# Gated linear attention with a squared-ReLU mixer on one core: the same operations in another order, from two new tables of plan positions

## The chip, the cores and the metric

The kernel runs on one core of one Trainium2 chip. The metric is the device time of one execution in microseconds (us). Before the change three executions took 425.59, 427.54 and 427.96 us, a median of 427.54. One more execution was taken with the hardware profiler; it took 424.87 us, and its trace has a span of 423.0 us.

## The reference

Two layers follow each other. The first is a linear attention whose state decays with a complex gate, for 4 batches, 8 heads, 768 positions and a head size of 48:

```python
mag = np.sqrt(a_re * a_re + a_im * a_im)
scale = np.minimum(mag, 0.999) / (mag + 1e-06)
for t in range(S):
    S_re, S_im = ar * S_re - ai * S_im + k[t] v[t]^T, ar * S_im + ai * S_re
    y[:, :, t] = q[t] @ S_re
```

The second takes the attention's output `x` (768 positions of 384 features for each batch):

```python
x_prev = x shifted by one position
xk, xr = mu_k * x + (1 - mu_k) * x_prev, mu_r * x + (1 - mu_r) * x_prev
k = np.maximum(xk @ w_k, 0.0)            # 384 -> 1024
v = k * k @ w_v                          # 1024 -> 384
out = v / (1.0 + np.exp(-(xr @ w_r)))    # 384 -> 384
```

All is float32.

## The kernel before

**Units.** A batch is cut into two halves of 384 positions, which gives eight units u = 0 to 7. A unit goes through three groups of steps.

- *gate(u)* loads the gate, k and q in three pieces of 128 features (`g`, line 673) and v (`v`, line 682). ScalarE (ACT) and VectorE (DVE) turn the gate into a log magnitude and a phase, sum both along the positions and multiply k and q by the results. ACT needs two of its function tables for it (exponential and logarithm, then arctangent and sine) and a third for the sigmoid later on; each change is an ACT_TABLE_LOAD (line 304). The last products of a gate are `g<-g,r` on DVE (line 808).
- *attend(u)* does the attention in chunks of 128 positions. SyncE (SP) copies k and q of each head from `g` into a head's own tile (`kq`, line 845; unit 0 also uses `x`). TensorE (PE) turns k round (`tr`, line 876), ACT copies that out (`kt`, line 882), PE makes the state's increments (`up`, line 896), DVE adds them up (lines 901 and 903). PE makes the scores (`sc`, line 925), DVE masks them (`pt`, line 934), and PE makes the output of a pair of heads (`y`, lines 960 and 966), which ACT copies out (`ys`, line 975) and SP moves into the mixer's input (`xt`, line 981).
- *mix(u)* takes differences of neighbours (`dx`, line 417) and mixes them (`xm`, line 435; for unit 0 straight into `x`, line 425). A float32 operand goes through PE as a high and a low part, three products in the place of one: ACT makes the high part (`x`, line 443), DVE the low (line 446). `z` (line 464) is the product with w_k or w_r; ACT takes ReLU (`r`, line 500) and the square (`h`, line 504), ACT or DVE the square's high part (`hhi`, line 326), DVE its low (`hlo`, line 512); `o` (line 531) is the product with w_v, added up over eight steps j. DVE multiplies by the gate (line 553) and SP stores. Unit 0 uses undivided float32 weights and operands in the place of the parts: `z` on line 459 and `o` on line 528.

**Weights** come in ten pieces in a packed form (`raw`, line 384), ACT or DVE takes the exponent out (line 600), DVE shifts and joins (lines 606 and 610), and after unit 0's use they are split into high and low parts (`w`, lines 633 and 636). All ten loads are needed for unit 0, the later steps j last.

**Looks.** Each of the 19 weight blocks is loaded once more (`again`, line 649) into a single buffer, DVE masks it (line 653), and ACT measures it (lines 655 and 656); the sums decide at the end whether a slow path has to run. As there is one buffer, the load of a look cannot begin before ACT has ended the look before it.

**Fillers.** While PE has nothing ready early in the program, the order holds small products of the identity (`warm`, line 1019). Their number is fixed when the program is built.

**What sets the order.** All operations are first recorded, with an estimated cost, in a `Plan`. `AT` holds for each unit's attend and mix a stretch on a line of plan time, over which its PE operations are spread evenly (`steps`); `SHIFTS` moves the due times of everything that is not on PE, one number for each call of `run`. `due` works back from PE's places to a due time for each operation; `Plan.run` then plays the plan through, and at each moment each engine takes, of the operations that could start, the one that is due first:

```python
i = min((i for i in queue if can(i)), default=None,
        key=lambda i: (due[i] + self.STAY * (e == "PE" and ops[i]["kind"] != kind), i))
```

The instructions are written out in the order in which the plan took them. On the chip each engine's queue, SP's too, runs strictly in that order: an instruction that waits holds up all behind it on its engine. In the same way all transfers are issued from SP, one after another. Which of ACT and DVE makes a `hhi`, or takes out an exponent, is also decided in the play.

Of the kernel before, what the change touches and what calls it, by code (L numbers as in the profile page):

```python
# [41 lines left out]
CAP = 0.999  # L42


AT = ((0.0, 16.0), (6.28, 13.76), (7.74, 9.08), (13.58, 23.34), (8.72, 9.63), (16.36, 26.91), (19.37, 20.41), (27.64, 32.72),
      (27.54, 33.34), (28.23, 33.79), (27.95, 29.17), (65.85, 145.98), (25.53, 63.88), (108.62, 138.07), (34.95, 105.45), (30.5, 41.58))
SHIFTS = (9.3, 16.4, 21.7, 11.3, 10.8, -22.0, 2.7, 0.8, 22.0, -13.5, 2.3, 36.2, 2.3, -15.3,
          12.9, 19.7, -32.6, 0.0, 0.5, 0.5, 1.2, -6.4, 0.0, 0.2, -54.6, 2.7, 50.3, 46.6)
PAIRS = 0, 3, 1, 2
PIECE = 2  # L50
GP = 2
# [234 lines left out]
def tile_kernel(ctx, tc, gat, vt, w_all, mu, slow_g, slow_v, out):  # L286
# [275 lines left out]
    with ExitStack() as fast:  # L562
# [460 lines left out]
        n = range(len(pieces))  # L1023
        shifts = iter(SHIFTS)
        run(gate(0), 0, 0, next(shifts))
# [3 lines left out]
        for u in range(NU):  # L1029
            run(attend(u), *AT[2 * u], next(shifts))  # L1030
            run(mix(u, (x0, x0_slot) if u == 0 else None), *AT[2 * u + 1], next(shifts))
            if u == 0:
# [151 lines left out]
```

## Time and profile before

| | |
|---|---|
| three executions, us | 425.59, 427.54, 427.96 (median 427.54) |
| profiled execution, us | 424.87 |
| its span, us | 423.0 |
| busy in the span, us | PE 379.8, weight loads 346.9, ACT 350.0, DVE 329.0 |
| moved by DMA | 69.92 MB, 16 engines busy 55% of the span on the kernel's queue |
| table loads on ACT | 22 |

The profile's page has the busy share of each engine in 40 slices, the chain of waits that ended last, and the costliest groups. The view of waits names for each engine the operation that waited, the one it waited for, the total, the number of times and the longest. The view of stretches gives busy time of each engine between two moments. PE's records of a plain float32 product are two for one matmul, so 82 records of `warm` are 41 fillers.

### The profile page before, as it was taken

What the parts mean: (1) busy time and instruction counts of PE and PEld (TensorE: products, weight loads), DVE (VectorE), ACT (ScalarE), POOL (GpSimd) and SP (SyncE); (2) the same over time, 40 slices, a digit from 0 to 9 for tenths busy, and PEclk for the clock granted to TensorE, in tenths of its full rate; (3) what the DMA queues carried; (4) which work ended last, traced back from release to release, by engine and by line L of the source; (5) the groups of instructions that cost most, each with busy time, mean ns of one, the idle gap of its engine ahead of it and who ended that gap; (6) DMA issues with size and microseconds to landing.
All of it is one profiled execution on the core that took longest, in us unless ns stands there. A gap on an engine that the chain in (4) does not pass through costs nothing.

```text
span 423.0 us, 9454 instructions
## 1 busy us (share of the span) xinstructions
PE 379.8 (90%) x3655; PEld 346.9 (82%) x3655; DVE 329.0 (78%) x522; ACT 350.0 (83%) x635; POOL 6.3 (1%) x40
## 2 busy tenths in 40 slices
PE   1007999999999999999999999999999999999993
PEld 1007985676779998999999998998899999999992
DVE  6799889988699989699979787959978865356421
ACT  5899979686999899899998999889999954675431
POOL 3000000000000000000000000000001000000000
PEclk9999999999999999999999999999999999999998
DMA  7958899249727555594659363846442635314101
GB/s 277 416 209 186 277 313 288 59 125 297 169 59 245 174 134 143 150 325 123 112 153 332 92 166 100 278 174 146 129 113 84 142 94 150 102 40 130 39 2 64
DMA packets 28661, 69.92 MB, mean 165 GB/s; under 512 B 5696, under 2 KB 11840, under 8 KB 28608
## 3 DMA queue, kind: packets, MB, share of 16 engines
q1 hardware_dynamic: 28608, 69.23, 55.3%
q8 instruction: 31, 0.51, 0.5%
q14 instruction: 22, 0.18, 0.2%
HBM read 40.90 MB, written 4.72 MB: 108 GB/s over the span
## 4 chain that ended last, share of the span: by engine, by line
PE 67%; ACT 13%; DMA 10%; DVE 6%; SPq 2%; issue 1%; DVEq 0%; ACTq 0%
PE z L464 26%; PE o L531 16%; PE sc L925 6%; PE y L960 5%; PE up L896 4%; PE y L966 4%; DMA g<-in_gat 3%; PE tr L876 3%; DMA raw<-in_w_all 2%; PE z L459 2%; PE o L528 2%; DMA again<-in_w_all 2%; ACT r L310 2%; DVE g L808 2%; ACT L304 2%; DMA xt<-ys 1%
## 5 line engine op out<-in xcount | busy, mean ns | idle before, releaser
L464 PE MATMUL z<-x,w 128*128 128x384 f32 x693 | 133.3, 340 | 0.0
L464 PEld LDWEIGHTS z<-x,w 128*128 128x128 f32 x693 | 120.3, 188 | 1.8 <-issue 1.2
L531 PE MATMUL o<-hhi,w 128*128 128x384 f32 x336 | 87.4, 341 | 0.0
L531 PEld LDWEIGHTS o<-hhi,w 128*128 128x128 f32 x336 | 60.0, 188 | 0.8 <-issue 0.5
L531 PE MATMUL o<-hlo,w 128*128 128x384 f32 x168 | 56.8, 338 | 0.9 <-DVE hlo L512 0.9
L876 PE MATMUL tr<-ident,g 128*128 128x128 f32 x120 | 19.4, 287 | 30.6 <-DVE g L808 30.6
L808 DVE TENSOR_TENSOR g<-g,r 128x768 f32<-128x768 f32 x48 | 42.8, 953 | 5.1 <-ACT r L310 4.8
L500 ACT ACTIVATE r<-z 128x384 f32<-128x384 f32 x64 | 30.8, 484 | 19.0 <-PE z L464 17.4
L876 PEld LDWEIGHTS tr<-ident,g 128*128 128x128 f32 x120 | 14.0, 144 | 33.3 <-DVE g L808 31.6
L925 PEld LDWEIGHTS sc<-kq 112*64 112x64 f32 x744 | 33.4, 137 | 3.6 <-issue 3.2
L925 PE MATMUL sc<-kq 112*64 112x64 f32 (+1 forms) x744 | 36.0, 249 | 0.0
L504 ACT ACTIVATE h<-r 128x384 f32<-128x384 f32 x64 | 33.1, 523 | 0.8
L934 DVE TENSOR_TENSOR pt<-sc,masks 128x512 int32<-128x512 int32 x48 | 31.3, 684 | 2.2 <-PE sc L925 2.2
L531 PEld LDWEIGHTS o<-hlo,w 128*128 128x128 f32 x168 | 31.5, 188 | 1.5 <-DVE hlo L512 1.5
L310 ACT ACTIVATE sq<-m 128x1152 f32<-128x1152 f32 (+2 forms) x30 | 27.9, 967 | 5.6 <-DVE m L756 5.6
L512 DVE TENSOR_TENSOR hlo<-h,hhi 128x384 fp32r<-128x384 f32 x56 | 30.4, 553 | 2.0 <-ACT hhi L326 0.5
L304 ACT ACT_TABLE_LOAD x22 | 28.2, 1283 | 1.1 <-PEq L1173 0.8
L446 DVE TENSOR_TENSOR x<-xm,x 128x384 fp32r<-128x384 f32 x42 | 23.2, 552 | 5.9 <-ACT x L443 5.9
L960 PE MATMUL y<-pt,v 128*64 128x128 f32 (+1 forms) x384 | 27.3, 276 | 0.0
L435 DVE SCALAR_TENSOR_TENSOR xm<-dx,mu_sb,xt 128x384 f32<-128x384 f32 x42 | 25.5, 615 | 0.9
L653 DVE TENSOR_SCALAR again<-again 128x384 uint8<-128x384 uint8 x19 | 11.5, 608 | 18.9 <-DMA again<-in_w_all 15.9
L443 ACT CAST x<-xm 128x384 fp32r<-128x384 f32 x42 | 21.0, 513 | 6.3 <-PE z L464 3.2
(85 smaller groups left out, 644.2 us busy)
## 6 DMA issues: line engine op xcount, KB each, us to landing
g<-in_gat SPq DMA_DIRECT2D x18, 768.0 KB, 6.2
kq<-g SPq DMA_DIRECT2D x94, 144.0 KB, 3.4
again<-in_w_all SPq DMA_DIRECT2D x19, 384.0 KB, 3.3
raw<-in_w_all SPq DMA_DIRECT2D x9, 768.0 KB, 8.7
v<-in_vt SPq DMA_DIRECT2D x24, 288.0 KB, 4.7
g<-in_gat SPq DMA_DIRECT2D x12, 384.0 KB, 6.7
out_t<-zr SPq DMA_DIRECT2D x24, 192.0 KB, 2.1
xt<-ys SPq DMA_DIRECT2D x48, 72.0 KB, 3.1
```

Source lines behind the costliest of these rows:

```text
L304: nc.scalar.add_instruction(mybir.InstLoadActFuncSet(name=nc.get_next_instruction_name(), act_func_set_id=loaded[0], engine=mybir.EngineTy ...
L310: nc.scalar.activation(out=out, in_=in_, func=func, **kw)
L464: nc.tensor.matmul(z, lhsT=wt[s[0]][:, part, s[1]], rhs=r[which][:, ct], start=n == 0, stop=n == 3 * NT - 1)
L500: nc.scalar.activation(out=t["r", j], in_=t["f", j], func=AF.Relu)
L504: nc.scalar.activation(out=t["h", j], in_=t["r", j], func=AF.Square)
L512: nc.vector.tensor_tensor(out=t["lo", j], in0=t["h", j], in1=t["hi", j].bitcast(F32), op=ALU.subtract)
L531: nc.tensor.matmul(tiles["o", mt], lhsT=wt[W_V + 2 * j][:, part, ts(mt, P)], rhs=r, start=j == 0 and n == 0, stop=j == NJ - 1 and n == 2)
L808: nc.vector.tensor_tensor(out=g[:, ct, 2 * i:2 * i + 2], in0=g[:, ct, 2:4], in1=t["r"][:, ct, 1 - i:2 - i].to_broadcast([P, 2, U]), op=ALU ...
L876: nc.tensor.transpose(out=t["tr", c, part][:, ct * P:(ct + 1) * P], in_=G[u][:, ct, 2 * part, c * P:(c + 1) * P], identity=ident)
L925: nc.tensor.matmul(sc[rows, i, cols], lhsT=kq[2 * p + j][:, 0, c * P + late * Q:][:, :Q], rhs=q if j else q[:, ::-1], start=True, stop=True)
L934: nc.vector.tensor_tensor(out=pts[k, c].bitcast(I32), in0=both, in1=masks.unsqueeze(1).to_broadcast([P, 2, 2, P]), op=ALU.bitwise_and)
L960: nc.tensor.matmul(t["y", p][rows, ts(c, P)], lhsT=V[u][c][:, cols], rhs=w, start=c == 0, stop=False)
```

## The change

Only the two tables of numbers are replaced. All operations, sizes, buffers and estimated costs stay as they are. The numbers were found by a search that took as its measure the mean over replays in which transfers land late by random amounts; those before went by the plan's length.

```diff
-AT = ((0.0, 16.0), (6.28, 13.76), (7.74, 9.08), (13.58, 23.34), (8.72, 9.63), (16.36, 26.91), (19.37, 20.41), (27.64, 32.72),
-      (27.54, 33.34), (28.23, 33.79), (27.95, 29.17), (65.85, 145.98), (25.53, 63.88), (108.62, 138.07), (34.95, 105.45), (30.5, 41.58))
-SHIFTS = (9.3, 16.4, 21.7, 11.3, 10.8, -22.0, 2.7, 0.8, 22.0, -13.5, 2.3, 36.2, 2.3, -15.3,
-          12.9, 19.7, -32.6, 0.0, 0.5, 0.5, 1.2, -6.4, 0.0, 0.2, -54.6, 2.7, 50.3, 46.6)
+AT = ((3.46, 6.82), (0.08, 10.89), (1.48, 1.99), (12.28, 20.43), (8.51, 12.78), (15.29, 21.97), (16.79, 17.69), (18.73, 25.2),
+      (21.73, 28.63), (22.46, 28.96), (20.36, 23.11), (71.92, 148.9), (21.27, 76.59), (101.4, 131.96), (58.71, 126.27), (37.6, 56.94))
+SHIFTS = (15.7, 108.1, 129.2, 35.2, 23.3, 17.2, -12.5, 37.4, 6.1, 0.4, -29.4, -0.4, 4.5, 0.0,
+          4.8, -5.6, -5.6, 1.2, -6.5, -1.4, 3.9, 6.0, -62.0, -11.1, -30.6, -1.6, 76.5, 5.6)
```

What it moves is seen in the engines' orders. The fillers go from 55 to 52; 41 of them stood in one row ahead of unit 0's first `z`, and 33 stand there now. Of the `hhi`, 22 were on DVE and 24 are now. The number of table loads is the same. Three places follow.

**SP, from the last moves of unit 0's k and q to the loads ahead of unit 1's.** `raw` are weight pieces, `g` the gate pieces of unit 2, `xt` the parts of unit 0's attention output, `v` values, `kq` unit 1's k and q. Before:

```order
L384 DMA raw<-in_w_all 128x6144 x2
L981 DMA xt<-ys 48x384 x2
L981 DMA xt<-ys 32x384
L981 DMA xt<-ys 16x384
L673 DMA g<-in_gat 128x1536
L981 DMA xt<-ys 16x384
L981 DMA xt<-ys 32x384
L673 DMA g<-in_gat 128x1536 x2
L981 DMA xt<-ys 48x384 x4
L682 DMA v<-in_vt 128x576 x3
L384 DMA raw<-in_w_all 128x6144 x3
```

Now:

```order
L384 DMA raw<-in_w_all 128x6144 x2
L673 DMA g<-in_gat 128x1536
L981 DMA xt<-ys 48x384 x2
L981 DMA xt<-ys 32x384
L981 DMA xt<-ys 16x384 x2
L981 DMA xt<-ys 32x384
L673 DMA g<-in_gat 128x1536
L981 DMA xt<-ys 48x384 x4
L673 DMA g<-in_gat 128x1536
L682 DMA v<-in_vt 128x576 x3
L384 DMA raw<-in_w_all 128x6144
```

The last four moves of `xt` have two pieces of `g` ahead of them in the place of three. The last two weight pieces are issued after the 14 moves of unit 1's first heads (`kq`), no longer ahead of them.

**ACT, between the sigmoid of unit 0 and unit 3's gate.** The table load is the one back to the exponential's table, after the last sigmoid (`zr<-zr`) of unit 0; `kt` are the copies for unit 2's state, two for each chunk. Before:

```order
L882 COPY kt<-tr 128x8x48 x2
L443 CAST x<-xm 128x384 x2
L482 COPY zr<-z 128x384
L633 CAST w<-raw 128x2x384
L310 ACTIVATE zr<-zr 128x384
L304 ACT_TABLE_LOAD
L310 ACTIVATE m<-m,consts 128x1152
L633 CAST w<-raw 128x2x384
L310 ACTIVATE ph,stat<-m 128x1152
L443 CAST x<-xm 128x384
L882 COPY kt<-tr 128x8x48
L633 CAST w<-raw 128x2x384
```

Now:

```order
L882 COPY kt<-tr 128x8x48 x2
L443 CAST x<-xm 128x384 x2
L633 CAST w<-raw 128x2x384
L482 COPY zr<-z 128x384
L882 COPY kt<-tr 128x8x48 x2
L443 CAST x<-xm 128x384
L633 CAST w<-raw 128x2x384
L310 ACTIVATE zr<-zr 128x384
L304 ACT_TABLE_LOAD
L310 ACTIVATE m<-m,consts 128x1152
```

The second chunk's two copies stand ahead of the table load and of the gate's two long functions.

**DVE, at the end of unit 6.** `again` are the looks, `hhi` and `hlo` the parts of the squares that unit 6's `o` reads, `x`, `xm` and `dx` the making of unit 7's operands. Before, from one look to the next but one:

```order
L653 TENSOR_SCALAR again<-again 128x384
L446 TENSOR_TENSOR x<-xm,x 128x384
L435 SCALAR_TENSOR_TENSOR xm<-dx,mu_sb,xt 128x384
L326 CAST hhi<-h 128x384
L512 TENSOR_TENSOR hlo<-h,hhi 128x384
L653 TENSOR_SCALAR again<-again 128x384
L446 TENSOR_TENSOR x<-xm,x 128x384
L435 SCALAR_TENSOR_TENSOR xm<-dx,mu_sb,xt 128x384
L417 TENSOR_TENSOR dx<-xt 128x384
L446 TENSOR_TENSOR x<-xm,x 128x384
L512 TENSOR_TENSOR hlo<-h,hhi 128x384
```

Now, from the look at the same place:

```order
L653 TENSOR_SCALAR again<-again 128x384
L446 TENSOR_TENSOR x<-xm,x 128x384
L435 SCALAR_TENSOR_TENSOR xm<-dx,mu_sb,xt 128x384
L446 TENSOR_TENSOR x<-xm,x 128x384
L435 SCALAR_TENSOR_TENSOR xm<-dx,mu_sb,xt 128x384
L326 CAST hhi<-h 128x384
L417 TENSOR_TENSOR dx<-xt 128x384
L512 TENSOR_TENSOR hlo<-h,hhi 128x384
L446 TENSOR_TENSOR x<-xm,x 128x384
L435 SCALAR_TENSOR_TENSOR xm<-dx,mu_sb,xt 128x384
L512 TENSOR_TENSOR hlo<-h,hhi 128x384
```

Four instructions stood between that look and the next; now twelve do (the last two are not shown), and the parts for two steps of `o` (`hlo`) are among them.

## The prediction

> **What bounds the kernel now.** I read the page first, then the stretches, then the waits of TensorE (PE), and last the timelines at the places where PE waits.
>
> ```profile
> span 423.0 us, 9454 instructions
> PE 379.8 (90%) x3655; PEld 346.9 (82%) x3655; DVE 329.0 (78%) x522; ACT 350.0 (83%) x635; POOL 6.3 (1%) x40
> ...
> PE tr L876 <- DVE g L808: 30.6, 3, 26.8
> PE up L896 <- ACT kt L882: 1.9, 3, 0.9
> PE o L531 <- DVE hlo L512: 0.9, 2, 0.4
> PE o L528 <- ACT h L504: 0.5, 1, 0.5
> PE z L459 <- DVE x L425: 0.4, 1, 0.4
> ...
> PE tr L876 <- DVE g L808: 0.3, 1, 0.3
> ```
>
> PE is the fullest engine, and three quarters of its idle time is one wait: the first `tr` waits until ACT and DVE have made unit 0's gate. The other waits come to 0.3 + 1.9 + 0.9 + 0.5 + 0.4 = 4.0 us (0.3 is the last row, the same wait asked for after 60 us alone; the rest of its 30.6 lies at the start). By stretches (columns: from:to, length, busy PE, weight loads, DVE, ACT, POOL, granted clock, DMA share, GB/s):
>
> ```profile
> 34.00:61.50 27.50, 27.40 (x393) 26.54 (x394) 24.71 (x37) 24.71 (x52) 0.00 (x0) 1.00 0.86 256
> 61.50:119.00 57.50, 56.51 (x476) 37.60 (x474) 50.70 (x73) 48.69 (x78) 0.24 (x1) 1.00 0.67 185
> 119.00:280.00 161.00, 159.80 (x1629) 152.49 (x1630) 139.11 (x221) 150.45 (x267) 0.73 (x2) 1.00 0.61 179
> 280.00:303.00 23.00, 21.94 (x217) 20.62 (x216) 20.17 (x34) 22.33 (x41) 0.00 (x0) 1.00 0.45 106
> 303.00:374.00 71.00, 71.00 (x708) 68.07 (x707) 47.82 (x82) 54.06 (x109) 1.96 (x13) 1.00 0.43 115
> 374.00:386.00 12.00, 11.15 (x62) 10.51 (x61) 7.60 (x16) 7.58 (x18) 0.00 (x0) 1.00 0.22 66
> 416.00:423.00 7.00, 0.00 (x0) 0.00 (x0) 0.45 (x2) 0.00 (x0) 0.00 (x0) 0.75 0.29 97
> ```
>
> From 34 us on PE is busy nearly without a break, until 416; then 7 us of end follow. So the time is 34 us of start, the work of PE, what PE loses inside, and 7 us. An order changes neither the work nor the end. The new order does not change the start either: ACT's order is the same up to the Exp of unit 1's gate, and DVE's up to the second of the six `g<-g,r` of unit 0, after which one join (`raw`, line 610) stands in the place of two shifts. What can be won lies inside: the 4.0 us of waits, and the fillers, which count as busy:
>
> ```profile
> 34.58 1.49 PE L1019 MATMUL warm<-ident 128*128 128x128 f32 x6
> ...
> 52.25 9.42 PE L1019 MATMUL warm<-ident 128*128 128x128 f32 x82
> ```
>
> 82 records in 9.42 us are 0.115 us each, or 0.23 us a filler.
>
> **Term A: from the first attention output to unit 0's first products.** The 41 fillers from 52.25 stand for a wait: unit 0's first `z` (line 459) needs `x` on DVE (line 425), that needs `dx` (line 417), and that the last moves of `xt`.
>
> ```profile
> 45.98 2.45 SPq L981 DMA_DIRECT2D xt<-ys  x4
> ...
> 50.48 2.00 SPq L673 DMA_DIRECT2D g<-in_gat  x2
> 53.83 3.15 SPq L981 DMA_DIRECT2D xt<-ys  x4
> ...
> DMA to landing us min/median/max: 4.9/5.5/6.9
> ...
> 52.15 8.28 DMA g<-in_gat
> ...
> 61.14 1.03 DVE L417 TENSOR_TENSOR dx<-xt 128x384 f32<-128x384 f32 x2 [1.08 <-DMA v<-in_vt]
> ...
> xt<-ys SPq DMA_DIRECT2D x48, 72.0 KB, 3.1
> ```
>
> These ten moves of 24 to 72 KB took 4.9 to 6.9 us to land; the median of the whole run is 3.1 for the 72 KB ones. The last two `dx` began at 61.14, 0.7 us after the third piece of `g` (768 KB, 52.15 + 8.28 = 60.43) had landed. The name beside the wait is v's; I take it to be the last `xt`, which DVE needs, and v it does not. The change puts that piece of `g` behind the four moves. Of 5.5 us of landing I take 2 off, towards the 3.1 (5.5 - 3.1 = 2.4 at most): `dx` then begins near 59. The order agrees: it has eight fillers fewer in that row and five more ahead of it, three fewer in all, 0.7 us.
>
> The Trainium skill has the rule for it (DMA: Bandwidth & Descriptors, Queues, rings and completion order): on each DMA engine the descriptors of a ring are consumed in the order of the ring. By that rule a piece of `g` issued later could not delay these moves at all, and they would gain the piece's whole time. The landings of 4.9 to 6.9, against 3.1 elsewhere, fit it.
>
> With `x` earlier, the two waits behind it go: `z` L459 (0.4) because `dx` comes 2 us earlier against 0.7 fewer fillers, and `o` L528 (0.5) because the order now puts unit 1's first two `tr` between unit 0's third `z` and its first `o`. That is 0.7 + 0.4 + 0.5 = 1.6. The weight loads ahead of the same two products waited longer:
>
> ```profile
> PEld z L459 <- DVE x L425: 1.3, 2, 1.0
> PEld o L528 <- ACT h L504: 1.1, 1, 1.1
> PEld o L531 <- DVE hlo L512: 1.5, 2, 0.8
> ```
>
> With 1.3 and 1.1 it is 3.1. I take 1.9, near the lower, as a wait of a weight load is partly under the matmul before it. Bounds: 0 (if `x` comes no earlier, fewer fillers only make a longer wait) to 3.1.
>
> **Term B: the copies for unit 2's state.**
>
> ```profile
> 113.44 1.28 ACT L304 ACT_TABLE_LOAD   x1
> 114.74 1.26 ACT L310 ACTIVATE m<-m,consts 128x1152 f32<-128x1152 f32 x1
> 116.62 1.16 ACT L310 ACTIVATE ph<-m 128x1152 f32<-128x1152 f32 x1
> 119.28 0.47 ACT L882 COPY kt<-tr 128x384 f32<-128x384 f32 x1
> ...
> 119.81 1.13 PE L896 MATMUL up<-v,kt 128*64 128x48 f32 x32 [0.86 <-ACT kt L882]
> ```
>
> The copies now stand ahead of 1.28 + 1.26 + 1.16 us of table load and gate. PE in turn asks for `up` earlier: unit 0's last four operations `o`, some 4 us of PE's work, now stand behind it. ACT's copies come by the three long ones and one split (0.8) earlier, 4.5 us, so the wait of 0.86 goes. Bounds: 0, and 0.86; I take 0.9. The other two of the three waits for `kt` I leave.
>
> **Term C: the looks.**
>
> ```profile
> DVE again L653 <- DMA again<-in_w_all: 15.9, 9, 3.6
> ...
> 377.29 0.61 DVE L653 TENSOR_SCALAR again<-again 128x384 uint8<-128x384 uint8 x1 [2.97 <-ACT x L443]
> ...
> 380.50 0.44 PE L531 MATMUL o<-hlo,w 128*128 128x384 f32 x1 [0.43 <-DVE hlo L512]
> 382.77 0.44 PE L531 MATMUL o<-hlo,w 128*128 128x384 f32 x1 [0.42 <-DVE hlo L512]
> ```
>
> DVE waited 15.9 us in nine looks whose load was not there. Mostly that costs nothing. At 374.3 it did: DVE stood 2.97 us at a look, the `hlo` behind it came late, and PE lost 0.43 + 0.42 there (1.5 by the weight loads). In the new order both `hlo` stand ahead of the next look. I take 1.2, between 0.9 and 1.5; bounds 0 and 1.5.
>
> At 280 to 303 PE lost 23.00 - 21.94 = 1.06, behind two more waits of DVE for looks. One of the two looks stands where it stood; the other's load is now issued ahead of three loads of v. I take 0.3, bounds 0 and 1.06.
>
> **Term D: new waits.** Elsewhere PE asks earlier than before: for unit 1's outputs `y` (6.8 us of PE's work earlier), for unit 2's (8.1), unit 3's first `tr` (2.3), while DVE's producers come 4.6, 5.0 and 0 us earlier in DVE's own order (both counted by the operations that changed sides, at their mean times). From 119 to 280 ACT has 150.45 busy of 161 and DVE 139.11, so neither has much to catch up with. Nothing in the trace prices this; bounds are 0 and once more all small waits of today, 4.0. I take 1.0: DVE's 22 free us there are near enough.
>
> **Sum.** -1.9 - 0.9 - 1.2 - 0.3 + 1.0 = -3.3 us. On the profiled execution: 424.87 - 3.3 = 421.6 (span 419.7, with the same 1.9 around it). That execution is 2.7 us under the median of the three shown, and those span 2.4, so I set the difference against the median: 427.54 - 3.3 = **424.2 us**. With all bounds at their ends: 427.54 - 3.1 - 0.9 - 1.5 - 1.1 = 420.9, and 427.54 + 4.0 = 431.5.
>
> **Rivals.** *Given back.* A, B and C happen, but ACT and DVE, at 93% and 86% from 119 to 280, set the pace there, and PE waits for them what it has gained ahead: only C and 0.3 are left, with 1.0 new: 427.0. For it: those shares. Against: PE's 159.80 of 161, so today they do keep up; and the sum of ACT's work falls by two `hhi`.
>
> *Slower: the late weight pieces.* The last two pieces were issued at 61 and are now issued after unit 1's moves.
>
> ```profile
> L384 SPq DMA_DIRECT2D raw<-in_w_all x10: 327/328/583, 9.2 to 61.3; - x10
> ...
> DMA to landing us min/median/max: 4.4/9.2/11.4
> ...
> 71.89 4.12 SPq L845 DMA_DIRECT2D kq<-g  x6
> 75.17 1.50 DVE L606 TENSOR_SCALAR raw<-raw 128x768 int32<-128x768 int32 x3
> ```
>
> In the old times the moves end at 76.0; 2 to 2.5 us earlier the pieces go out at 73.5 to 74. DVE, which now takes the exponent out of one itself, reaches it near 76.5 (75.17 + 0.5, with three masks and two state sums put ahead, 3.0, and 2 us earlier). Landing after 4.4 means 78 and 1.5 us of wait, which DVE hands on to unit 1's second `y`, within D. Landing after 9.2 means 83 and 6.5 us, of which PE sees about 6. The point from which it decides is about 7 us of landing. A PE that idles so long also runs slow afterwards: six records of fillers took 1.49 us at 34.58, 0.25 each against 0.115, and that lasted until about 37.8, which costs some 1.6 us. Sum: 427.54 - 3.3 + 6 + 1.6 = 431.8. For it: 9.2 is the median. Against: those loads queued behind others, and at 74 only small moves are ahead.
>
> The Trainium skill states the slow rate as a clock gate (TensorE: Matmul & The Clock Gate, Part 1): after an idle window of about 3.4 us PE's clock is halved, and a busy window brings it back. The fillers at 34.58, after 26.8 us of waiting, agree in size, though the clock column shows 1.00 there.
>
> *More.* Nothing new waits and C's other looks pay too: 427.54 - 3.1 - 0.9 - 1.5 - 1.1 = 420.9.
>
> **Chances.** The forecast 0.45, given back 0.27, slower 0.15, more 0.13. About 0.5% (2.1 us) is what a measurement of this kernel tells from no change. Under 425.4 lies most of the forecast's case and all of "more": 0.56. Within 0.5%: given back, and the forecast's upper edge: 0.29. Slower: 0.15. The forecast's own range is 422.0 to 426.0; for eight in ten I go to 419.0 and 429.0, which leaves out half of the slower case and a little below.
>
> **What would show it.** A: the last two `dx` begin before 60, `z` L459 no longer stands among PE's waits, and the four last moves of `xt` land in 3 to 4 us. B: no wait of `up` near 119. C: DVE's wait for `again` falls well below 15.9 us, and no wait of `o` L531 near 380. D: the sum of PE's small waits stays under 2.5 us. The prediction is wrong if that sum is 4 or more, if DVE waits over 3 us for `raw` near 77, or if the start is no longer 34 us.

## The result, and the profile after

The new order took 425.14 us in the median (18 executions), the old one 427.38 us (18 executions beside them): a ratio of 0.995, 95% interval 0.9928 to 0.9972, or 2.2 us less. The forecast was 424.2, 3.3 us less. The profiled execution took 423.19 us, with a span of 421.5 (before: 424.87 and 423.0).

The page's head:

```profile
span 421.5 us, 9448 instructions
PE 380.0 (90%) x3649; PEld 347.0 (82%) x3649; DVE 330.2 (78%) x522; ACT 347.4 (82%) x635; POOL 7.3 (2%) x40
```

PE's waits after 60 us (engine, line, what it waited for: us in total, times, longest):

```profile
PE sc L925 <- DMA kq<-g: 0.6, 2, 0.5
PE o L531 <- DVE hhi L326: 0.5, 1, 0.5
PE o L531 <- DVE hlo L512: 0.5, 2, 0.3
PE o L528 <- ACT h L504: 0.5, 1, 0.5
```

The waits for `kt`, for the first `x` and for unit 6's `g` are gone, 4.0 us of waits have become 2.1, and two of the four rows are new (`sc` and `hhi`). The same stretches as before, with the same columns:

```profile
34.00:61.50 27.50, 27.50 (x389) 26.28 (x390) 26.16 (x41) 25.62 (x53) 0.57 (x1) 1.00 0.76 227
61.50:119.00 57.50, 56.39 (x520) 38.80 (x518) 49.96 (x71) 47.52 (x76) 0.00 (x0) 1.00 0.69 198
119.00:280.00 161.00, 161.00 (x1596) 152.92 (x1593) 138.69 (x216) 149.97 (x270) 1.15 (x2) 1.00 0.60 174
280.00:303.00 23.00, 23.00 (x266) 21.83 (x267) 20.86 (x35) 22.60 (x43) 0.00 (x0) 1.00 0.55 138
303.00:374.00 71.00, 71.00 (x666) 68.02 (x663) 47.55 (x83) 50.16 (x101) 2.27 (x13) 1.00 0.43 110
374.00:386.00 12.00, 11.02 (x60) 10.01 (x59) 8.48 (x18) 8.62 (x20) 0.00 (x0) 1.00 0.22 56
```

From 119 to 374 PE has no idle time left (it had 1.20 + 1.06). From 374 to 386 it is idle for 0.98, more than before (0.85).

A busy share hides small gaps, and one profile is one execution. The experiments below leave most of the program alone, so each of their profiles is another sample of the old or the new order outside its own edit. For each I took the start of a named product and subtracted the usual time (the median from one start to the next, by kind of product, in the old order's profile) of all PE's products ahead of it, fillers left out. What remains is the start of the program, fillers and gaps; how it grows from one named product to the next is PE's loss in that stretch:

| PE's loss in us, stretches not edited | old order | new order | means |
|---|---|---|---|
| start to unit 2's first `sc` (near 112) | 47.8, 49.9, 48.2, 50.6, 47.3 | 47.6, 48.4, 48.0 | 48.7 to 48.0: -0.7 |
| to unit 2's first `z` of `mix` (near 170) | 1.7, 1.9, 2.1, 2.5 | 1.0, 2.3, 1.3, 2.6, 2.0, 1.1, 2.1, 1.8 | 2.1 to 1.8: -0.3 |
| to unit 5's first `z` (near 302) | 3.1, 2.1, 3.3, 2.6 | 1.0 in all eight | 2.7 to 1.0: -1.8 |
| to unit 7's first `z` (near 383) | 2.0, 1.5, 1.5, 1.9, 2.5 | 2.8, 3.0, 2.5, 2.6 | 1.9 to 2.7: +0.8 |

The sum is -2.0, near the measured -2.2. It also shows where executions of one order differ: by up to 3.3 us before 112 us, by 1.6 at most in any later stretch. Only the third row lies clear of that spread; the fourth touches it, and the first two lie within it.

### The profile page after: what moved, and what is told of

It is laid out like the page before. It is cut to its first block, busy times and chain, and to the rows that moved or that the text cites. A ratio compares the mean times of both kernels' runs of the same rounds, so it can differ in the third digit from the quotient of the medians.

```text
span 421.5 us, 9448 instructions
## 1 busy us (share of the span) xinstructions
PE 380.0 (90%) x3649; PEld 347.0 (82%) x3649; DVE 330.2 (78%) x522; ACT 347.4 (82%) x635; POOL 7.3 (2%) x40
## 4 chain that ended last, share of the span: by engine, by line
PE 78%; DMA 7%; DVE 5%; ACT 5%; issue 2%; SPq 1%; ACTq 0%; DVEq 0%
PE z L464 27%; PE o L531 18%; PE sc L925 8%; PE y L960 5%; PE up L896 4%; PE y L966 4%; PE z L459 4%; PE o L528 3%; PE tr L876 3%; DMA raw<-in_w_all 2%; DMA xt<-ys 2%; DMA again<-in_w_all 2%; DMA kq<-g 1%; DMA g<-in_gat 1%; PE warm L1019 1%
## 5 line engine op out<-in xcount | busy, mean ns | idle before, releaser
L531 PE MATMUL o<-hhi,w 128*128 128x384 f32 x336 | 88.0, 343 | 0.5 <-DVE hhi L326 0.5
L531 PEld LDWEIGHTS o<-hhi,w 128*128 128x128 f32 x336 | 59.6, 188 | 2.1 <-DVE hhi L326 1.0
L531 PE MATMUL o<-hlo,w 128*128 128x384 f32 x168 | 56.8, 338 | 0.5 <-DVE hlo L512 0.5
L925 PE MATMUL sc<-kq 112*64 112x64 f32 (+1 forms) x744 | 37.0, 250 | 0.6 <-DMA kq<-g 0.6
L925 PEld LDWEIGHTS sc<-kq 112*64 112x64 f32 x744 | 33.9, 137 | 4.2 <-issue 2.9
L531 PEld LDWEIGHTS o<-hlo,w 128*128 128x128 f32 x168 | 31.6, 188 | 1.2 <-DVE hlo L512 1.1
L960 PEld LDWEIGHTS y<-pt,v 128*48 128x48 f32 (+1 forms) x384 | 21.1, 130 | 4.9 <-issue 1.8
```

Of the source, the lines that this page charges most:

```text
L531: nc.tensor.matmul(tiles["o", mt], lhsT=wt[W_V + 2 * j][:, part, ts(mt, P)], rhs=r, start=j == 0 and n == 0, stop=j == NJ - 1 and n == 2)
L925: nc.tensor.matmul(sc[rows, i, cols], lhsT=kq[2 * p + j][:, 0, c * P + late * Q:][:, :Q], rhs=q if j else q[:, ::-1], start=True, stop=True)
L960: nc.tensor.matmul(t["y", p][rows, ts(c, P)], lhsT=V[u][c][:, cols], rhs=w, start=c == 0, stop=False)
```

## The experiments

All record the same operations and play the plan of one of the two orders. Then single operations are put elsewhere in their own engine's queue, ahead of the one named; a small function behind the loop of `Plan.run` does it, and the emission keeps each engine's queue, the dependences and the number of buffers. It shifts the line numbers in their profiles by 45 (by 51 in experiments 5 and 8). The diffs name the operations. A gap of PE is the time from one start to the next beyond the usual one, the slower product right behind it included; so it is longer than the wait in brackets, which runs from an end to a start. Ratios are against the old order measured beside the experiment.

**1. Term A alone, in the old order.**

```diff
 SP   xt x4 (last moves)
+SP   g unit 2, third piece      (stood ahead of the four moves)
 DVE  dx x2, x x2 (unit 0, first product)
+DVE  g, r of unit 1             (lines 764 and 793, stood ahead)
-PE   warm x8
```

> The old order with term A alone: on SP the third gate piece of unit 2 (g, line 673) stands behind the last four moves of xt, on DVE one product of unit 1's gate (g, line 764) and one split (r, line 793) stand behind unit 0's first x, and 8 of the 41 fillers in the long row are left out. Theory (the piece delays the moves): the four moves land in 3 to 4 us, the last two dx begin by 59.8, unit 0's first z starts at 59.7 and loses under 0.3 us inside; PE is 2.4 us ahead there (1.8 of fillers, 0.6 of wait), and 1.0 to 2.4 us of it reach the end. Rival 1 (the moves are slow by themselves): dx stays near 61.1, z waits 1.8 us more, time as before within 0.5 us. Rival 2 (given back at once): dx is early, but o (line 528) or the first scores sc of unit 1 wait as much longer, time as before within 0.5 us.

Measured: ratio 1.0031 (1.0005 to 1.0058), slower. The moves landed after 2.1 to 3.7 us (5.1 to 6.9 in the old order), both `dx` ran from 57.88, and the first three `z` ran without a gap, 2 us earlier. Then PE stood, and afterwards it ran slowly. PE's rows, and ACT's, in the experiment's timeline (start, us, engine and line; in brackets the idle time before):

```profile
59.61 5.97 PE L504 MATMUL z<-x,raw 128*128 128x384 f32 x18
69.36 4.21 PE L573 MATMUL o<-h,raw 128*128 128x384 f32 x6 [3.78 <-ACT h L549]
...
61.20 1.16 ACT L753 ACTIVATE m<-g 128x1152 f32<-128x1152 f32 x1 [1.81 <-DMA g<-in_gat]
64.83 1.28 ACT L349 ACT_TABLE_LOAD   x1
67.28 0.47 ACT L545 ACTIVATE r<-z 128x384 f32<-128x384 f32 x1
```

The ReLU (line 500 before) stands in ACT's queue behind the first function of unit 2's gate, which needs all three pieces of `g`, and behind a table load. A later piece of `g` holds up ACT there, and so did my own edit: `r` (line 793) came later, and ACT's functions of unit 1's gate with it. So the transfer theory holds for `dx`, and rival 2 for the place: what is won ahead of `z` is lost ahead of `o`. The time is 1.3 us longer, more than rival 2's 0.5, for the wait has a price behind it. The stretch that follows it, with the columns of the stretches above (the granted clock is the third number from the end):

```profile
70.00:74.00 4.00, 4.00 (x9) 2.22 (x8) 3.99 (x8) 3.88 (x7) 0.00 (x0) 0.50 1.05 174
```

PE's granted clock was 0.50 there, and the six records of `o` took 4.21 us; in the old order's profile they took 2.20.

**2. Term B alone, in the old order.**

```diff
+ACT  kt x2 (unit 2, second chunk)
 ACT  w (cast), ph (unit 3's gate), x (cast)
```

> The old order with term B alone: on ACT the two copies kt of unit 2's second chunk (line 882) stand one long function of unit 3's gate and two casts earlier. Theory: the wait of up at 119.8 (0.86 us, a gap of 1.0 between products) goes, and nothing else in PE's waits changes: 0.9 to 1.0 us faster. Rival (given back): the wait goes, but the next products wait for ACT's or DVE's later work; 0 to 0.4 us faster.

Measured: 0.9992 (0.9965 to 1.0019). The gap at 119 is gone, but the third chunk's `up` then waited 0.2 us, and the other two waits for `kt` stayed (1.0 us in all). The interval runs from 1.5 us faster to 0.8 slower, so the time does not decide between the theory (0.9 to 1.0) and the rival (0 to 0.4).

**3. Two looks later, in the old order.**

```diff
-DVE  again (wait of 2.23)        ACT  again x2
 DVE  r, dx, hhi, hlo             ACT  h, m, r, r
+DVE  again                      +ACT  again x2
-DVE  again (wait of 2.55)
 DVE  g<-g,r x6, hlo x2
+DVE  again
```

> The old order with two looks moved: DVE masks the looks that made it wait at 277.7 (2.2 us) and 283.2 (2.6 us) two and eight instructions later, and ACT measures them later; nothing else moves. Theory (the looks held DVE, DVE held the last products of unit 6's gate, and these held tr, up): g (line 808) of unit 6 is made 2.5 to 3 us earlier, PE's three gaps between 289 and 301 (0.39 + 0.37 + 0.77 = 1.5 us) go, 1.3 to 1.5 us faster. Rival 1 (ACT's gate functions set the pace there): the gaps stay, time as before within 0.4 us. Rival 2 (the looks come back later): the same gaps stand behind a look further on, time as before within 0.4 us.

Measured: 0.9991 (0.9965 to 1.0017). The first look moved past four instructions of DVE, not two as the expectation has it; ACT's measure of the second moved later as well. DVE's two waits for looks are gone, and PE's first two gaps there (0.39 + 0.37), but `up` now waits 1.2 in the place of 0.6, and DVE stands for other things:

```profile
282.08 0.56 DVE L462 TENSOR_TENSOR dx<-xt 128x384 f32<-128x384 f32 x1 [1.60 <-DMA xt<-ys]
286.71 1.83 DVE L853 TENSOR_TENSOR g<-g,r 128x768 f32<-128x768 f32 x2 [2.62 <-ACT r L355]
...
284.13 0.64 ACT L700 ACTIVATE again<-again,consts 128x384 f32<-128x384 uint8 x1 [1.28 <-DVE again L698]
```

The 2.62 is in part my edit: ACT's measure of the look, at its new place ahead of the gate's last two functions, waited 1.28 for DVE. So this says only that taking the looks from DVE's queue is not enough there.

**4. Term C alone, as it was forecast, in the old order.**

```diff
-DVE  again (wait of 2.97 at 374.3), and the three looks behind it
 DVE  x, xm, dx, x, hlo, x, hhi, xm, xm, hlo, x, hlo, x
+DVE  again (each look at the next one's place; on ACT and SP too)
```

> The old order with term C as it was forecast: the look at which DVE stood 2.97 us from 374.3, and the three looks behind it, each take the place of the next one; nothing else moves. Forecast's theory (the look held DVE, so hlo came late): the two waits of o (line 531) at 380 and 383 go, 0.9 to 1.35 us faster. Rival, from the profile of the new order, in which DVE stands 2.82 us in the same place at x (line 446) and no look is there: DVE cannot go on before ACT has cast unit 7's x (line 443), which comes behind ACT's own queue; DVE then waits at line 446 until about 377, the waits of o stay within 0.4 us of their 1.35, time 0 to 0.4 us faster.

Measured: 0.997 (0.9938 to 1.0001). DVE's row where the look had stood, and the same place in the new order, where the look is eight instructions further on:

```profile
376.17 0.56 DVE L446 TENSOR_TENSOR x<-xm,x 128x384 fp32r<-128x384 f32 x1 [2.82 <-ACT x L443]
```

In the experiment:

```profile
380.31 0.56 DVE L491 TENSOR_TENSOR x<-xm,x 128x384 fp32r<-128x384 f32 x1 [2.85 <-ACT x L488]
```

The look's own 0.4 us and one of PE's two gaps (0.69) went, the other (0.66) stayed. The look was the name of the wait, not its cause: without it DVE stands as long at `x`, whose high part ACT has not made. That cast, at 379.76, had itself waited 0.53 us for PE's last `z` of unit 6. The time, 1.3 us less with an interval from 2.6 less to none, does not decide between theory and rival; of PE's gaps each has about half.

**5. The parts ahead of that `x`, in the new order.**

```diff
+DVE  hhi, hlo x3 (unit 6, last three steps; two of the hhi were ACT's)
 DVE  x (line 446, wait of 2.82)
```

> The new order, with one place altered: ahead of the x (line 446) at which DVE stood 2.82 us from 373.4, DVE makes the parts hhi and hlo of the squares for the last three steps of unit 6's o, which were ready by 373.4; two of these hhi were ACT's. Theory (DVE's queue stood at unit 7's x, for which ACT's cast came late, and the parts behind it were not late themselves): the three gaps of o (line 531) at 376 to 382, 0.64 + 0.69 + 0.43 = 1.76 us, go; 1.3 to 1.8 us faster than the new order, 0.7 to 1.0% faster than the old (ratio near 0.991). Rival (unit 7's first z is the limit there, not o): the gaps of o go, but z (line 464) waits for x by as much; ratio as for the new order, 0.995.

Measured: 1.0026 (1.0005 to 1.0046) against the old order, some 0.8% slower than the new one. My theory fell, and so did its premise that the parts could be made at 373.4. DVE's and PE's rows:

```profile
377.52 0.36 DVE L377 CAST hhi<-h 128x384 fp32r<-128x384 f32 x1 [0.86 <-PE o L582]
379.10 0.36 DVE L377 CAST hhi<-h 128x384 fp32r<-128x384 f32 x1 [0.55 <-PE o L582]
...
386.39 1.04 PE L515 MATMUL z<-x,w 128*128 128x384 f32 x3 [1.87 <-ACT x L494]
```

Two of the three `hhi` wait for PE's `o`: the kernel has two buffers for `hhi`, so one comes free only with the `o` of two steps earlier. So three parts in a row pace DVE at PE's own speed, all of unit 7's `x` stand behind them, and PE's gaps move from `o` to `z` and grow from 1.8 to 2.9 us. Behind the wait of 1.87 PE then loses 1.5 us more, as its granted clock is halved:

```profile
387.50:390.50 3.00, 3.00 (x11) 3.00 (x10) 1.94 (x4) 1.66 (x5) 0.00 (x0) 0.50 0.51 109
```

**6. Unit 0's second `o` ahead of unit 1's scores, in the new order.**

```diff
+PE   o (unit 0, second step, line 528)
 PE   sc x3 (unit 1, line 925), up
+ACT  r, h (unit 0, first step)
 ACT  table load, m (unit 2's gate)
```

> The new order, with two edits between 63 and 77 us: PE does unit 0's second o (line 528) ahead of unit 1's first scores (sc, line 925), and ACT does the ReLU and the square of unit 0's first step ahead of the table load and the second long function of unit 2's gate. Theory (PE asks for unit 1's k and q before they have landed, and h stands in ACT's queue behind the gate): the gap ahead of o (0.59) goes, the gap in sc (1.36) falls under 0.5; 0.8 to 1.5 us faster than the new order, ratio to the old near 0.992. Rival (the moves of k and q set the pace until unit 1's first y): what is won is waited for at y (line 960); ratio 0.995.

Measured: 0.9921 (0.9892 to 0.9951). PE has no wait at all from 60 to 130 us. The theory holds in place. Against the new order's 0.995 it is 0.3% or 1.2 us, the size expected, but the two intervals overlap; the profile agrees, as by the measure of the table PE loses 1.8 us less up to unit 2's first `sc` than in the new order's own profile.

**7. One weight piece more behind unit 1's moves, in the new order.**

```diff
-SP   raw (eighth piece)
 SP   kq x14 (unit 1)
+SP   raw (eighth piece)
 SP   raw x2
 ACT  that piece's exponent (line 600) and DVE's shift (line 606) later too
```

> The new order, with one weight piece more behind unit 1's 14 moves of k and q: raw (line 384) that was issued at 60.4 goes out at 72 with the other two, and ACT and DVE take it up accordingly later. In the new order the eighth transfer after it, a move of k and q, waited 2.1 us on SP for that piece to land (SP waits for line 384's transfer at line 845). Theory (a transfer cannot be issued before the eighth one ahead of it has landed, as completion is counted by eight semaphores used in turn): that wait of 2.1 goes, the last six moves go out 1.5 to 2 us earlier, the gap in sc (line 925, 1.36) falls under 0.4; 0.7 to 1.3 us faster than the new order, ratio near 0.992. Rival (the moves wait for bandwidth or for DVE's g): SP waits as long for something else, gap in sc as before, ratio 0.995. Second rival (the late piece is now waited for): DVE or ACT stands at raw near 80, PE at y or z behind it; ratio above 0.995.

Measured: 0.9938 (0.9918 to 0.9958). SP's wait in the new order, its 14 moves there, and its 14 moves in the experiment:

```profile
SPq L845 <- DMA raw<-in_w_all: 2.1, 1, 2.1
```

```profile
62.19 11.34 SPq L845 DMA_DIRECT2D kq<-g  x14
```

```profile
62.56 8.77 SPq L890 DMA_DIRECT2D kq<-g  x14
```

The wait for `raw` is gone, the last move goes out at 70.8 and not at 73.0, and so is the gap in `sc` (1.36 us). The new order's records name the semaphore that each transfer waits for ($S) and the one that it signals:

```
60.38 DMA_DIRECT2D 429 $S[106]>= semaphore=106 dst_num_elem=[128,1] dst_elem_size=6144 384 raw<-in_w_all
66.23 DMA_DIRECT2D 582 $S[105]>= semaphore=105 dst_num_elem=[48,1] dst_elem_size=3072 845 kq<-g
68.89 DMA_DIRECT2D 504 $S[106]>= semaphore=106 dst_num_elem=[48,1] dst_elem_size=3072 845 kq<-g
```

All 348 transfers use eight semaphores strictly in turn, and none is issued before the eighth ahead of it has landed. The move at 68.89 could go no earlier than the landing of the piece issued eight transfers before it, 8.5 us after its issue. The theory holds for the wait and the gap. The time it saved is not told from the new order's: `o` (line 528) waited 0.7 for `h` in the place of 0.5, and further on unit 3's `tr` waited 0.5 for DVE's gate.

**8. Several at once, with fewer fillers, in the new order.**

```diff
 the edits of 5 and 7, ACT's h of unit 0 as in 6 and its r one function earlier; PE's o as it was
-PE   warm x4
```

> The new order with the edits at unit 6's o and with the weight piece behind the moves, ACT's ReLU and square of unit 0's first step ahead of the gate's first long function, and four of the 33 fillers in the long row left out. Theory (each of these waits is PE's own time): 1.5 + 1.0 + 0.6 + up to 0.9 = 3 to 4 us faster than the new order, ratio to the old near 0.987. Rival (what is won early is given back at unit 1's scores): only the 1.5 at unit 6 is left, ratio 0.991 to 0.992.

Measured: 0.9952 (0.9925 to 0.9978), above what either theory or rival named. The parts of experiment 5 cost as much here: a wait of 1.87 us at unit 7's `z`, and then 3.4 us at a granted clock of 0.50. What the four fillers did:

```profile
60.47 5.98 PE L510 MATMUL z<-x,raw 128*128 128x384 f32 x18
67.28 0.44 PE L927 MATMUL tr<-ident,g 128*128 128x128 f32 x2 [0.41 <-DVE g L859]
```

`z` begins earlier and has what it needs, but unit 1's first `tr` waits for DVE's last `g` of unit 1. So what the fillers gave ahead of `z` is in part waited for at once; DVE's last products of the gate do not let PE go sooner.

**9. The copies `kt` at all three places, in the old order.**

```diff
+ACT  kt x2 (unit 2), kt (unit 5), kt x2 (unit 6)
 ACT  gate functions, table load, casts
```

> The old order with ACT's copies kt (line 882) moved at all three places where PE's up waited for them: unit 2's second chunk as in the second experiment, unit 5's second copy ahead of one cast, unit 6's second chunk ahead of the table load and gate functions of unit 7. Theory (each of these waits is PE's own time): the gaps ahead of up at units 2, 5 and 6 (1.0 to 1.5, 0.54, 0.7 to 1.3 in the profiles so far) go, 2.0 to 2.8 us faster than the old order, ratio near 0.994; PE's loss between unit 2's second mixing product and unit 5's first, which was 2.1 to 3.7 us in the old order's profiles and 0.97 in the new one's, falls to about 1.5. Rival (given back): the copies come early, but the next y or z waits; ratio 0.998 to 1.000.

Measured: 0.9972 (0.9943 to 1.0000). The three gaps are gone, but the next chunk's `up` waits (0.49 at unit 2, 0.77 at unit 6), and unit 6's first `tr` waits 0.7 for DVE's `g` (0.3 in the old order's profile); the loss between unit 2's and unit 5's first `z` is 2.5 us, against 2.7 in the mean and 2.1 to 3.3 in single profiles. Theory and rival each explain a part; most was given back.

**10. ACT's cast for unit 7 earlier, in the new order.**

```diff
+ACT  x (unit 7, line 443)
 ACT  zr (sigmoid), zr (copy), zr (sigmoid) of unit 6
```

> The new order with one cast moved: ACT makes unit 7's x (line 443), for which DVE stood 2.82 us, ahead of the two sigmoids and one copy of unit 6 (lines 310 and 482), 1.3 us earlier. Theory (ACT's own queue makes that cast late; its buffer is free from the last z of unit 6, 374.05): DVE goes on 1.3 us earlier, the three gaps of o (line 531) at unit 6's end, 1.76 us, fall to 0.3 to 0.7, and unit 7's first z does not wait; 1.0 to 1.4 us faster than the new order, ratio near 0.992. Rival (the buffers of hhi and hlo, or unit 7's x, bind there, as when the parts were put first): the gaps stay or move to z; ratio 0.995 or more.

Measured: 0.9953 (0.9924 to 0.9981), no different from the new order in time, though its profile agrees with the theory. DVE's row, and PE's waits from 360 on:

```profile
375.12 0.56 DVE L491 TENSOR_TENSOR x<-xm,x 128x384 fp32r<-128x384 f32 x1 [1.78 <-ACT x L488]
```

```profile
PE o L576 <- DVE hlo L557: 0.4, 2, 0.2
```

DVE waits 1.78 in the place of 2.82, the gaps fall from 1.76 to 0.9, and the loss from unit 5's to unit 7's first `z` from 2.7 in the mean to 1.9. That is under what these executions can tell in time, with 3 us of spread ahead of 112 us.

**11. The edits of 6 and 7 together, in the new order.**

```diff
+PE   o (unit 0, second step)     ahead of unit 1's sc
+ACT  r, h (unit 0, first step)   ahead of the table load
+SP   raw (eighth piece)          behind unit 1's kq (on ACT and DVE as in 7)
```

> The new order with both sets of edits of the early part: unit 0's second o ahead of unit 1's scores with ACT's ReLU and square ahead of the gate, and the weight piece behind unit 1's moves. Theory (each repairs the same wait for k and q, plus the one for h): no gap over 0.3 us from unit 0's first z to unit 1's first y; as good as the better one alone or 0.3 us better, ratio 0.991 to 0.993. Rival (the late weight piece is now waited for): a gap at y or z behind 80 us, ratio 0.994 or more.

Measured: 0.9914 (0.9884 to 0.9943). As good as the better one; from 60 to 130 us a single wait of 0.2 is left (`y` for `pt`).

**12. The edits of 10 and 11 together, in the new order.**

```diff
 the edits of 11
+ACT  x (unit 7, line 443)        ahead of unit 6's sigmoids
```

> The new order with the edits of the tenth and the eleventh experiment together: unit 0's second o ahead of unit 1's scores, ACT's ReLU and square ahead of the gate, the weight piece behind unit 1's moves, and unit 7's cast ahead of unit 6's sigmoids. Theory (waits at places so far apart add up): 1.5 us for the early part and 0.9 us for unit 6's end, 2.4 us faster than the new order, ratio to the old near 0.990; PE's loss between unit 5's first and unit 7's first product is 1.9 us in place of 2.5 to 3.0. Rival (what is won early is waited for later): ratio 0.992 to 0.995, with a gap that no profile of the new order has shown so far.

Measured: 423.24 us against 427.21 of the old order beside it, 0.9906 (0.9877 to 0.9935), the fastest of all. PE's waits after 60 us:

```profile
PE tr L921 <- DVE g L853: 0.5, 1, 0.5
PE o L576 <- DVE hlo L557: 0.4, 2, 0.2
PE y L1005 <- DVE pt L979: 0.2, 1, 0.2
```

The loss from unit 5 to unit 7 is 1.9 again. So the places add up in the profile; the time cannot tell it from experiment 11's 0.9914, and its interval still overlaps the new order's (0.9928 to 0.9972) by a little. The 0.5 at unit 3's `tr` came up in experiments 5, 7, 8 and 11 too: there unit 3's gate sets the pace next.

## Why the prediction was right, and where it was not

**The frame held.** PE sets the time; the first products began at 33.9 where 34 was expected; the time fell by small waits that went. Of the 4.0 us of waits 2.1 are left, under the 2.5 that was named as the bound. The time lies 0.9 us above the forecast, in its own range; the saving is 0.52%, on the edge of what counts as faster, so the case "given back" was nearly as good a description as the forecast. That the sum came out near is in good part luck: A gave less than was said, C nothing, and the largest part came from waits that the sum had at nothing or at 0.3.

**Term A (-1.9) was too large; the table shows -0.7 up to unit 2's scores, which is within the spread of the old order's profiles there.** The transfers did more than was said: the last four moves landed in 2.1 to 3.0 us (3 to 4 was named), and the last `dx` began at 59.06 and 59.7. DVE's row and PE's fillers:

```profile
59.06 1.18 DVE L417 TENSOR_TENSOR dx<-xt 128x384 f32<-128x384 f32 x2
...
53.58 7.63 PE L1019 MATMUL warm<-ident 128*128 128x128 f32 x66
```

The Trainium skill's rule of the ring's order (DMA: Bandwidth & Descriptors, Queues, rings and completion order) fits these landings: with one 768 KB piece fewer ahead, they fell by 3 to 4 us.

But PE asks when the fillers are through, and their number is fixed: `z` began 0.46 earlier, no more. The step that failed is "the two waits behind it go". The wait of `z` (0.4) stands in no other profile of the old order, so it was no price of that order. The wait of `o` (0.5) stayed, as `h` stands in ACT's queue behind unit 2's gate and a table load; experiment 1 shows a wait of 3.78 there, and a slow PE after it. And a wait came that the old order's one profile did not show, for k and q:

```profile
73.04 0.43 PE L925 MATMUL sc<-kq 112*64 112x128 f32 x2 [0.17 <-DMA kq<-g]
73.93 1.74 PE L925 MATMUL sc<-kq 112*64 112x128 f32 x36 [0.46 <-DMA kq<-g]
```

These moves were late in the old order as well: gaps of 0.3, 2.2, 0.6, 3.1 and 0 us at the same place in its five profiles. So this wait is a cost of both orders, and the one profile of before showed little of it.

**Term B (-0.9): the wait went, the time hardly.** No `up` waits in the new profile. In experiment 2 this alone gave nothing that the time can tell, and the stretch it lies in fell by 0.3 only: new waits, at unit 1's `o` or unit 3's `tr`, stand there in five of the new order's eight profiles, though not in its own.

**Term C (-1.2) was wrong.** Its check is half right: DVE's wait for `again` fell from 15.9 to 8.3 us, yet `o` L531 waits near 376 to 382 as before, and the loss there rose by 0.8. The step that failed is "DVE stood 2.97 us at a look, the `hlo` behind it came late". The row that the prediction shows names ACT's cast of `x` as what ended that wait, and the 15.9 us of waits for loads do not contain it; the view has it by itself:

```profile
DVE again L653 <- ACT x L443: 3.0, 1, 3.0
```

The look's load, issued at 373.7, landed 3.2 us later, at about the time at which ACT had cast unit 7's `x` (377.1), which the next instruction needed; experiment 4 took the look away and the wait stayed, experiment 10 moved ACT's cast, in the new order, and it shrank by 1.0.

**The 0.3 for 280 to 303 was far too small, and term B left two waits out.** The stretch from unit 2's to unit 5's first `z`, whose end it is, gave 1.8, the largest part of the saving and the steadiest: 1.0 us of loss in all eight profiles. PE's waits in the old order's profile from 170 to 310:

```profile
PE up L896 <- ACT kt L882: 1.0, 2, 0.6
PE tr L876 <- DVE g L808: 0.3, 1, 0.3
```

In all four of the old order's profiles `up` waits for `kt` near 255 and near 300, and in two of them unit 6's first `tr` waits for DVE's `g`. As gaps these make 1.1 to 2.3 us, nearly all by which the two orders differ there; in none of the new order's eight profiles does PE wait in this stretch. So the step that failed is "The other two of the three waits for `kt` I leave": they were put at nothing, and they went. The looks were not what PE waited for; only the `tr` stands behind DVE's queue. Which moves took the waits away is not settled. Moving the copies alone (experiment 9) left 2.5 us, as `tr` and the next `up` then waited, and moving two looks alone (experiment 3) gave nothing. In the new order unit 6's gate runs 1.4 us earlier on ACT from 268 on, and its last products on DVE begin 3.4 us earlier. The rows before and after:

```profile
286.12 5.33 DVE L808 TENSOR_TENSOR g<-g,r 128x768 f32<-128x768 f32 x6
```

```profile
282.67 4.43 DVE L808 TENSOR_TENSOR g<-g,r 128x768 f32<-128x768 f32 x5
```

The looks, `kt` and PE's own order differ at once there; no run moved the gate and the copies together in the old order.

**Term D (+1.0)** had the right sign, but hardly the right places. Of those that it names, unit 3's `tr` waits 0.5 in five of the eight profiles, though not in the new order's own, and no `y` waits over 0.2. What unit 6's end lost (0.8) it does not name, and the wait of `sc` is a cost of both orders.

**The rival of the late weight pieces** did not come: the two pieces landed 5.2 and 7.2 us after their issue, ACT did wait 3.7 us for one (line 600), and DVE 0.2, but no PE product stood behind it for long. Experiment 7 put a third piece behind the moves, and no new wait of PE for a piece appeared. Its other half, that PE runs slowly after a long wait, is borne out by experiments 1, 5 and 8.

## What to carry to other kernels

A wait has as many causes as its queue has instructions behind it: before a wait is priced, ask what the next two instructions on that engine would wait for, and what the waiting engine asks for next. On a kernel whose PE is busy nine tenths, waits of 0.5 us are worth moving only where the next product is ready; that is found by moving the one operation and reading the profile, for the time cannot tell 1 us. A long wait costs more than itself: after 1.87 us PE lost another 1.5 at half its clock (experiment 5). And a single profile is one draw: stretches in which executions differ should be priced from several.

## What the runs showed of the hardware and had not been expected

In these programs every transfer on SP signals one of eight semaphores in turn, and none is issued before the eighth ahead of it has landed: the waiting is an instruction of the program's. A large load therefore holds up a small move eight places later: 2.1 us here. Where a long load stands modulo eight is part of the order.

The slow stage of PE after its long idle time does not have a fixed length. The same twelve records of fillers, in the new order's profile and in that of experiment 10:

```profile
36.27 1.85 PE L1019 MATMUL warm<-ident 128*128 128x128 f32 x12
```

```profile
36.55 2.77 PE L1064 MATMUL warm<-ident 128*128 128x128 f32 x12
```

In the first the slow rate ended within the row, in the second after it; `up`, behind them, still took 1.37 against 1.07 us. Since the fillers are a fixed number in a fixed order, all behind them shifts; that can be part of the 3.3 us by which executions differ ahead of 112 us. The clock column reads 1.00 in both, but only for want of a record: the trace's first record of the clock, a rise to 1.00, stands at 36.98 us in the first and at 39.94 in the second. The Trainium skill says why the stage's length varies (TensorE: Matmul & The Clock Gate, Part 1): the window over which activity is counted runs freely, so it depends on where in it the first product falls. The two rows agree, and no run here controls it.

Shorter waits in the middle of the program had the same effect. After a wait of 3.78 us (experiment 1) the granted clock was 0.50 for 6.8 us, and after waits of 1.87 us (experiments 5 and 8) for 3.4 us each; after the wait of 1.32 us in experiment 4 it stayed at 1.00. So less idle time than the 3.4 us that the prediction names was enough here, and the measurement decides.
